# Row maxima of an attention head computed four heads ahead of its scores instead of three

## The chip, the cores and the metric

The kernel runs on one core of a Trainium2 chip. The metric is the time of one execution in device microseconds (us); lower is better. The engines of the core work side by side, each through its own queue in order: PE (matrix multiply, with its weight loads shown as PEld), DVE (vector), ACT (activation functions), POOL (general purpose) and SP, which here issues all DMA transfers. They wait for one another through semaphores.

## What is computed

One transformer-like block on x of 2048 rows and 1024 columns, in fp32. A condition vector gives six modulation rows. Then comes a layer norm, an attention of 32 heads of width 32, a second layer norm and an MLP across the tokens. The attention works on four segments of 512 tokens, each with a causal softmax and with a running memory M, z of the segments before it:

```python
for s in range(N):
    qs, ks, vs = q[:, :, s], k[:, :, s], v[:, :, s]
    logits = jnp.einsum("bhqd,bhkd->bhqk", qs, ks) * scale + mask
    p = _softmax(logits, axis=-1)
    a_dot = jnp.einsum("bhqk,bhkd->bhqd", p, vs)
    pq = phi(qs)
    num = jnp.einsum("bhld,bhde->bhle", pq, M)
    den = jnp.einsum("bhld,bhd->bhl", pq, z)[..., None] + 1e-6
    o = g * (num / den) + (1.0 - g) * a_dot
    pk = phi(ks)
    M = M + jnp.einsum("bhld,bhle->bhde", pk, vs)
    z = z + jnp.einsum("bhld->bhd", pk)
x = x + ga * (o @ wo)
h = _layernorm(x, axis=-1) * (1 + cb) + sb
x = x + gb * mlp_over_tokens(h)
```

The softmax needs the largest logit of each row. This kernel computes the logits twice: once only to take the row maxima, and once more, transposed and with the maximum already subtracted, for the exponentials.

## The kernel before, in words

**Two large stages.** The attention stage lasts until about 1030 us, the MLP stage (lines 874 to 1102) from there to the end; the output product of the attention (line 791) joins them. The change touches the attention stage alone.

**Iterations and heads.** The attention runs over 32 iterations t (list `its`, line 362): two passes over pairs of segments, eight groups of four heads, two segments each. An iteration holds four heads h, so there are 128 heads in all, numbered n = 4t + h. Four kinds of work belong to an iteration:

- `project` (line 378) in four pieces. Pieces 0 and 1 multiply the normed tokens with the key and value weights (PE line 192, tile `nps`), 48 matmuls each. Piece 2 transposes the keys (line 405, `kps`), makes the queries (line 200, `qps`, 24 matmuls), splits both into a high and a low part in the tile `sg` (lines 119 and 122), and sends the parts of heads 0 to 2 with `stack` to the tiles `sk`. Piece 3 sends head 3, makes the values' parts `vp` and calls `memory` (line 441), which reads and updates the running memory (`rd` line 450, `up` line 460).
- `stack` (line 368): three DMAs of one head, lines 374 to 376, `sk<-sg`. There are two sets of `sk`, for even and odd t, so the stack of iteration t overwrites what the scores of iteration t-2 have read.
- `maxima` (line 468): the logits of a head in four matmuls (line 478, tiles `sx`, `sy`, `sz` in the two PSUM banks of tag `s1`), each with a reduction on DVE (line 480) into `mx`. After every second head PE transposes `mx` (line 486, `nmps`, in the only bank of tag `ms`), ACT and DVE make the negated maximum in two parts `nt` (lines 488, 489), and four DMAs write them as two further rows of the `sk` of both heads (line 493, `sk<-nt`).
- `scores` (line 507): four matmuls (lines 515, 518, 521, 522, tile `a`) on all 98 rows of `sk`, so that the maximum is subtracted inside the product; then exponentials on ACT (516, 519, 523), the causal cut on POOL (526), and a high part (528, ACT) and a low part (530, POOL) of the result. `values` (line 532) multiplies these with `vp` (line 544, `pv`) and reduces (547 to 554); after the fourth head the result is transposed (line 559, `ops`, again in the bank `ms`) and stored.

**The loop around the change** (lines 686 to 713) walks over steps n. In a step stand, in this order: the scores of head n, the maxima of head n + LEADS, the values of head n - 2, piece n + 8 of the projections (LEADP), reloads of stored weights and tokens, and planned extras (`plan`, line 590): loads of weights and their split, the norms of later tokens (`token_tile`, line 252), the modulation sums (`mod_late`, line 572, tile `rawm`), the preparation of the output weights. Some of the extras are to be issued on their engine behind a mark of the same step (`behind`, line 499): the last maximum of the step on DVE ("V"), the copy on ACT ("A"), the low part on POOL ("G"). `token_tile` and `mod_late` use the mark "V", which `maxima` sets:

```python
for n in range(-LEADS, 4 * NI + VL):
    at(scores, n)
    at(maxima, n + LEADS)
    at(values, n - VL)
    m = n + LEADP
```

**The order on the engines** isn't this order word for word. The context is opened with `schedule_with_timeline_sim=True` (line 1137): when the kernel is built, the instructions of each engine are put in order by a modelled timeline in which those that come earlier in the program have precedence among those that are ready. On the chip each engine then goes through its list in that fixed order and waits where something is late.

Of the kernel before, what the change touches and what calls it, by code (L numbers as in the profile page):

```python
# [26 lines left out]
SHIFT = 14.0 * math.log(2.0)  # L27
NV = 97
FT = F // P
LEADP, LEADS, NSK = 8, 3, 8  # L30
XB = 4
VL = 2
ML0 = 36
# [2 lines left out]
WOS = 6  # L36
WCT = 5
LEADP = 8
LEADS = 3


def attention_and_mlp(ctx, tc, x, wq, wkv, wo, beta, w1, b1, w2, b2, c, wm_a, wm_b, out):
# [425 lines left out]
    def maxima(t, h):  # L468
# [5 lines left out]
        for tiles in ((0, 1), (2,), (3,)):  # L474
# [4 lines left out]
            for i, o in outs:  # L479
                marks[4 * t + h - LEADS, "V"] = V.tensor_tensor_reduce(  # L480
                    o, o, mask[:, 384 - 128 * i:], 1.0, -3.0e38, op0=ALU.add, op1=ALU.max,
# [111 lines left out]
    def at(f, n):  # L593
        if 0 <= n < 4 * NI:
            f(n // 4, n % 4)
# [89 lines left out]
# [5 lines that stand above are left out]
# [451 lines left out]
```

## Time and profile before

| what | value |
| --- | --- |
| median of 3 runs | 2224.89 us |
| lowest and highest | 2224.09 and 2230.13 us |
| the profiled execution | 2226.6 us, of which its span on the core 2224.9 us |
| granted PE clock over the span | 0.997 |
| DVE, ACT and POOL busy | 1666.7, 1135.7 and 725.8 us |
| DMA | 423.03 MB, mean 190 GB/s |

A row of groups reads: line, engine, operation, out<-in with the program's names, shape, count, then busy time in us and the mean of one in ns, then the idle time of the engine just before them and what ended it. A row of waits reads: who waited, for whom, us in total, times, longest. Times in the timeline count from the start of the span.

### The profile page before, as it was taken

Reading aid. Unit: us, or ns where it says so; the run is one execution under the profiler, and the core shown is the slowest. Engines: PE = TensorE matmul, PEld = TensorE weight load, DVE = VectorE, ACT = ScalarE, POOL = GpSimd, SP = SyncE. Lnnn points to the kernel's source line nnn. Section 1 sums busy time; section 2 is a strip of 40 time slices with the busy share of each in tenths; the row PEclk is TensorE's granted clock in tenths of the full one; section 3 lists DMA queues with packets and bytes.
Section 4 is the critical chain, followed back from the end, with each engine's and each line's share of the span. In section 5 each row is a group of like instructions: output and inputs, shape, how many; then the busy total and the mean of one; then the engine's idle time right before and its main releaser. Section 6 shows DMA issues by size and latency. Waiting matters only on the chain.

```text
span 2224.9 us, 38052 instructions
## 1 busy us (share of the span) xinstructions
PE 2190.3 (98%) x13786; PEld 1881.0 (85%) x13786; DVE 1666.7 (75%) x3762; ACT 1135.7 (51%) x2050; POOL 725.8 (33%) x831
## 2 busy tenths in 40 slices
PE   8999999999999999999999999999999999999999
PEld 5988898888999999888888888888888888888887
DVE  7676777756777777664858766888888886969687
ACT  5486776756666666654636533533334242424232
POOL 2175766646767776663002200033330000000000
PEclk9999999999999999999999999999999999999999
DMA  7666666686556666664754687655556542414134
GB/s 287 192 187 191 175 181 193 189 279 216 170 180 205 188 183 211 193 219 143 231 194 186 226 304 275 243 223 220 204 202 219 206 148 64 145 57 147 57 123 151
DMA packets 175183, 423.03 MB, mean 190 GB/s; under 512 B 17524, under 2 KB 71828, under 8 KB 166036
## 3 DMA queue, kind: packets, MB, share of 16 engines
q1 hardware_dynamic: 174996, 420.61, 57.5%
q8 instruction: 109, 1.79, 0.3%
q14 instruction: 78, 0.64, 0.1%
HBM read 244.62 MB, written 125.06 MB: 166 GB/s over the span
## 4 chain that ended last, share of the span: by engine, by line
PE 87%; DVE 5%; DMA 3%; ACT 2%; POOL 1%; issue 1%; SPq 0%; DVEq 0%; ACTq 0%
PE mx L921 48%; PE nps L192 11%; PE po L791 8%; PE qps L200 7%; PE pv L544 3%; PE a L515 1%; PE sz L478 1%; PE sx L478 1%; DMA sk<-nt 1%; PE up L460 1%; PE a L518 1%; POOL p L530 1%; PE a L522 1%; PE sy L478 1%; PE rd L450 1%
## 5 line engine op out<-in xcount | busy, mean ns | idle before, releaser
L921 PE MATMUL mx<-bU,sp 128*128 128x512 f32 x2352 | 534.3, 389 | 0.9 <-DVE ac L928 0.9
L921 PEld LDWEIGHTS mx<-bU,sp 128*128 128x128 f32 x2352 | 441.3, 188 | 93.4 <-issue 1.3
L119 ACT CAST sp<-wr 128x384 fp32r<-128x384 f32 (+2 forms) x408 | 218.1, 547 | 431.8 <-PE mx L921 349.1
L192 PE MATMUL nps<-wv,h 128*128 128x256 f32 x3072 | 431.2, 283 | 1.6 <-DVE h L122 0.7
L921 PE MATMUL mx<-bA,sp 128*128 128x512 f32 x1764 | 430.5, 389 | 0.0
L530 POOL TENSOR_TENSOR p<-p,ph 128x640 f16<-128x640 f32 x256 | 380.2, 1485 | 138.5 <-ACT ph L528 134.5
L192 PEld LDWEIGHTS nps<-wv,h 128*128 128x128 f32 x3072 | 400.3, 189 | 9.4 <-DVE h L122 2.0
L921 PEld LDWEIGHTS mx<-bA,sp 128*128 128x128 f32 x1764 | 331.2, 188 | 68.7
L122 DVE TENSOR_TENSOR sp<-wr,sp 128x384 fp32r<-128x384 f32 (+2 forms) x408 | 259.8, 648 | 24.7 <-ACT sp L119 24.4
L928 DVE TENSOR_TENSOR ac<-mx,ac 128x512 f32<-128x512 f32 x280 | 189.9, 687 | 85.2 <-PE mx L921 84.1
L200 PE MATMUL qps<-h,wq 128*128 128x512 f32 x768 | 197.9, 400 | 0.0
L528 ACT CAST ph<-p 128x1280 f16<-128x1280 f32 x128 | 161.4, 1261 | 59.7 <-POOL p L526 59.6
L791 PE MATMUL po<-wo,ots 128*128 128x512 f32 x768 | 180.9, 391 | 0.0
L791 PEld LDWEIGHTS po<-wo,ots 128*128 128x128 f32 x768 | 142.7, 188 | 28.7
L200 PEld LDWEIGHTS qps<-h,wq 128*128 128x128 f32 x768 | 141.6, 190 | 27.7
L921 PE MATMUL mx<-bB,sp 128*128 128x512 f32 x588 | 164.0, 389 | 0.0
L526 POOL TENSOR_SCALAR_AFFINE_SELECT p<-p 128x256 f32<-128x256 f32 x256 | 134.1, 529 | 81.8 <-ACT p L523 53.9
L921 PEld LDWEIGHTS mx<-bB,sp 128*128 128x128 f32 x588 | 110.4, 188 | 22.9
L480 DVE CUSTOM_DVE_ANT_0 sz<-sz,mask 128x512 f32<-128x512 f32 x128 | 89.1, 696 | 52.0 <-PE sz L478 49.5
L480 DVE CUSTOM_DVE_ANT_0 sx<-sx,mask 128x128 f32<-128x128 f32 (+1 forms) x256 | 93.7, 366 | 44.1 <-PE sx L478 37.9
L928 DVE TENSOR_TENSOR cc<-mx,cc 128x512 f32<-128x512 f32 x140 | 94.9, 684 | 37.6 <-PE mx L921 37.4
L516 ACT ACTIVATE p<-a,shift 128x512 f32<-128x512 f32 x128 | 88.4, 691 | 41.2 <-PE a L515 40.4
(209 smaller groups left out, 3244.7 us busy)
## 6 DMA issues: line engine op xcount, KB each, us to landing
sk<-sg SPq DMA_DIRECT2D x384, 128.0 KB
wr<-in_w_dram SPq DMA_DIRECT2D x28, 1024.0 KB
wr<-in_w_dram SPq DMA_DIRECT2D x32, 768.0 KB
bstu<-ucd SPq DMA_DIRECT2D x28, 768.0 KB
wsp<-wv SPq DMA_DIRECT2D x32, 512.0 KB
rawm<-in_wm_b_dram SPq DMA_DIRECT2D x32, 512.0 KB
wv<-wsp SPq DMA_DIRECT2D x32, 512.0 KB
pcd<-cc SPq DMA_DIRECT2D x14, 1024.0 KB
```

What stands on the lines that cost most here:

```text
L119: last_hi[0] = A.copy(hi, src)
L122: return lo_eng.tensor_tensor(lo, src, hi.bitcast(F32), op=ALU.subtract)
L192: T.matmul(ps[:, aa], h[:, j, 128 * tt:128 * tt + 128], wt[:, i, o:o + 256], start=(n == 0), stop=(n >= 6 * NK - 2), skip_group_check=True)
L200: T.matmul(ps, wt[:, i, o:o + 128], h[:, j], start=(k + n == 0), stop=(3 * k + n == 3 * NK - 1))
L480: marks[4 * t + h - LEADS, "V"] = V.tensor_tensor_reduce(o, o, mask[:, 384 - 128 * i:], 1.0, -3.0e38, op0=ALU.add, op1=ALU.max, accum_out= ...
L516: A.activation(p32[:, 0:512], b0, AF.Exp, scale=SCALE, bias=shift)
L526: G.affine_select(w, w, pattern=[[0, 2], [1, 128]], compare_op=ALU.is_ge, fill=0.0, base=0, channel_multiplier=-1)
L528: marks[n, "A"] = A.copy(hi, p32)
L530: marks[n, "G"] = G.tensor_tensor(lo[:, c], p32[:, c], hi[:, c], op=ALU.subtract)
L791: T.matmul(ps, os_[:, i, P * ct:P * ct + P], wop[ct, nh][:, j], start=(n == 0), stop=(n == 3 * NK - 1))
L921: T.matmul(ps, ops[q][:, i, P * k:P * k + P], b[:, j], start=(m == 0 and first), stop=(m == 3 * nk - 1), skip_group_check=True)
L928: V.tensor_tensor(d, ps, d, op=ALU.add)
```

## The change

The lead of the maxima over the scores, LEADS, becomes 4:

```diff
@@ -27,7 +27,7 @@
 NV = 97
 FT = F // P
-LEADP, LEADS, NSK = 8, 3, 8
+LEADP, LEADS, NSK = 8, 4, 8
@@ -36,7 +36,7 @@
 LEADP = 8
-LEADS = 3
+LEADS = 4
```

The loop starts one step earlier, at n = -4, and that step holds only the maxima of head 0 and no projection. In every later step stand the maxima of head n + 4 instead of n + 3. No instruction is added or removed; the index of the mark "V" (`4 * t + h - LEADS`, line 480) still names the step in which the maximum stands. Buffers and banks stay as they are.

In the loop's text the maxima of head 0 of an iteration now stand two steps behind piece 2 of its projection (step 4t - 6 against 4t - 4) instead of three. The two heads with a transpose of `mx` (h = 1 and h = 3) fall on the steps in which n leaves 1 and 3 when divided by 4, where they fell on those that leave 2 and 0.

## The prediction

> **What bounds the kernel.** I read the page first, then the two stages, then PE's own waits in the attention stage.
>
> ```profile
> span 2224.9 us, 38052 instructions
> PE 2190.3 (98%) x13786; PEld 1881.0 (85%) x13786; DVE 1666.7 (75%) x3762; ACT 1135.7 (51%) x2050; POOL 725.8 (33%) x831
> PE 87%; DVE 5%; DMA 3%; ACT 2%; POOL 1%; issue 1%; SPq 0%; DVEq 0%; ACTq 0%
> PE mx L921 48%; PE nps L192 11%; PE po L791 8%; PE qps L200 7%; PE pv L544 3%; PE a L515 1%; PE sz L478 1%; PE sx L478 1%; DMA sk<-nt 1%; PE up L460 1%; PE a L518 1%; POOL p L530 1%; PE a L522 1%; PE sy L478 1%; PE rd L450 1%
> ```
> ```profile
> 60.00:1030.00 970.00, 950.20 (x8249) 864.27 (x8249) 688.30 (x2048) 636.92 (x1136) 612.63 (x717) 0.99 0.65 195
> 1030.00:2225.00 1195.00, 1190.41 (x5267) 984.75 (x5265) 934.52 (x1626) 466.77 (x862) 99.61 (x65) 1.00 0.51 181
> ```
> ```profile
> PE a L515 <- DMA sk<-nt: 4.1, 5, 1.4
> PE up L460 <- DVE am L454: 3.8, 3, 3.5
> PE a L521 <- ACT p L516: 2.4, 3, 1.0
> PE sy L478 <- DVE mx L480: 1.9, 2, 1.2
> ...
> PE sx L478 <- DMA sk<-sg: 0.2, 1, 0.2
> ```
>
> The columns of the two stretches (from the view of busy time by stretch) are length, then PE, PEld, DVE, ACT, POOL busy, the granted clock, the DMA share and GB/s. PE is the bound throughout: in the MLP stage it idles 1195.0 - 1190.4 = 4.6 us, in the attention stage 970.0 - 950.2 = 19.8 us. DVE, ACT and POOL have room in both (688, 637 and 613 us of 970). So the change can't shorten the work; it can only remove or add places where PE, going through its list in a fixed order, stands still. The waits that it aims at, scores that wait for the maxima's rows (`a L515 <- DMA sk<-nt`), are 4.1 us in five places of 128. The chain that ended last gives the same transfer 1% of the span, 22 us, but counts the whole flight of a transfer, with work of PE beside most of it; I keep it as the outer bound of a gain.
>
> **How far ahead the maxima really are.** The change names the program's order; the trace shows the engines' order.
>
> ```profile
> L478 PE MATMUL sx<-sk x256: 218/325/522, 62.4 to 988.7; 96*128 96x128 f32 x128
> L515 PE MATMUL a<-sk x128: 391/400/505, 98.5 to 1017.7; 98*128 98x512 f32 x128
> ```
>
> One head takes (1017.7 - 98.5) / 127 = 7.24 us. The first head's maxima run 98.5 - 62.4 = 36.1 us ahead of its scores, five heads; the last head's 1017.7 - 988.7 = 29.0 us, four heads. So the lead of three in the text is a lead of four to five on the engine. What holds the maxima from running still earlier is the arrival of the stacked queries and keys, as iteration 19 shows, with SP's queue first and PE's behind it:
>
> ```profile
> 613.51 0.68 SPq L374 DMA_DIRECT2D sk<-sg  x1
> 614.32 0.64 SPq L375 DMA_DIRECT2D sk<-sg  x1
> 615.41 2.65 SPq L493 DMA_DIRECT2D sk<-nt  x4
> 618.10 0.59 SPq L376 DMA_DIRECT2D sk<-sg  x1
> ```
> ```profile
> 623.74 0.22 PE L478 MATMUL sx<-sk 96*128 96x128 f32 x1
> ```
> ```profile
> 129.27 3.26 DMA sk<-sg
> ```
> ```profile
> 491.71 3.58 DMA sk<-sg
> ```
>
> The third stack DMA of head 0 is issued at 618.10; by the two pieces of the chain such a DMA lands 3.3 to 3.6 us after its issue, so at about 621.5, and the first maxima matmul starts at 623.74: 2.2 us of room. Between the first two and the third, SP issued four `sk<-nt` of an earlier pair, 2.65 us; the two kinds of transfer share the queue.
>
> **Part by part.**
>
> (a) *Scores no longer wait for `nt`.* The maxima of heads 1 to 3 can come up to one head, 7.24 us, earlier; their stacks land sooner than they are needed. Of the 4.1 us, the mean wait is 4.1 / 5 = 0.8 us. Bounds: 0 (SP's queue, below, decides when `nt` leaves) and -4.1. I take -3: four of five gone.
>
> (b) *Maxima of head 0 move up against their stack.* Room is 2.2 us, the move 7.24 us: followed to the letter, PE would stand 5 us in each of 31 iterations, 155 us. That is no likely end, because the list is made from a modelled timeline that puts other matmuls first while a stack isn't there; before, such waits came to 0.2 us in one place. But the matmul now stands as close behind its DMA as the model believes, 31 times, and the model doesn't see what SP is held by:
>
> ```profile
> SPq L493 <- ACT nt L488: 31.6, 12, 9.5
> ...
> SPq L374 <- PE a L522: 7.5, 7, 2.2
> ```
>
> SP stands for `nt` 12 times, up to 9.5 us, with the stacks of the next iteration, weight loads and stores queued behind it. With `nt` one head earlier in that queue, whoever is late there delays the stacks, and PE waits for those, with all matmuls of its list behind the waiting one. Bounds: 0 and 31 waits of the mean that the other maxima transfer shows, 0.8 us: 25 us. Between them I take a third of the places, 10 x 0.8 = +8.
>
> (c) *The bank `ms` is used in bunches.* Its users in turn were: `nmps` (steps with remainder 0 and 2), `ops` (1), two `rd` and one `up` (3). After, `nmps` stands in the steps of `ops` and of `rd`, `rd`, `up`, and the other two are empty. Each user must wait until DVE or ACT has read the one before; the row `up <- DVE am`, 3.8 us, is this wait. Bounds: 0 (the model spreads them) and one turn more in 32 iterations, the reading of `rd` in this row, 0.42 us, and a wait of the mean above, 0.8 us:
>
> ```profile
> L454 DVE TENSOR_TENSOR am<-rd,rdd 128x256 f32<-128x256 f32 x48 | 20.2, 420 | 0.7
> ```
>
> so at most 32 x 1.22 = 39 us. Nearest is the wait seen, and I let it double: +4.
>
> (d) *DVE work behind the mark "V".* The 32 modulation sums and eight token norms go one head later in DVE's list, because their mark is now the maximum of the next head. The timeline shows such a sum, 1.32 us, right behind its mark:
>
> ```profile
> 367.55 0.70 DVE L480 CUSTOM_DVE_ANT_0 sz<-sz,mask 128x512 f32<-128x512 f32 x1 [2.08 <-PE sz L478]
> ...
> 368.45 1.32 DVE L573 SCALAR_TENSOR_TENSOR rawm<-rawm,scb 128x1024 f32<-128x1024 f32 x1
> ```
>
> Their loads get 7 us more to land, but their three buffers (tag `raw`, shared with the weight loads) are held as much longer. Where this has mattered is the largest stop of the stage:
>
> ```profile
> 449.51 1.92 DVE L573 SCALAR_TENSOR_TENSOR rawm<-rawm,scb 128x1024 f32<-128x1024 f32 x1 [1.55 <-DMA rawm<-in_wm_b_dram]
> ```
> ```profile
> 455.29 1.00 PE L460 MATMUL up<-v,pk 128*128 128x132 f32 x3 [3.48 <-DVE am L454]
> ```
> ```profile
> 450.00:460.00 10.00, 6.53 (x47) 5.92 (x46) 9.08 (x20) 6.25 (x13) 5.03 (x9) 0.69 1.03 361
> 460.00:470.00 10.00, 10.00 (x60) 8.35 (x59) 5.53 (x16) 4.60 (x8) 7.27 (x7) 0.80 0.91 323
> ```
>
> A modulation sum waited for its load, two weight splits stood behind it, then the reading of the memory's bank for which `up` waits, and PE stood for 3.48 us. After that the granted clock was 0.69 and 0.80 over two stretches of 10 us, which loses 10 x 0.31 + 10 x 0.20 = 5.1 us more. One such stop costs 8.6 us. The new order may lose this one (-8.6) or make another (+8.6); no row says which, so I take 0 and keep both.
>
> ```profile
> 130.00:140.00 10.00, 9.22 (x68) 8.06 (x67) 7.21 (x13) 8.63 (x15) 6.87 (x9) 0.83 0.99 264
> ```
>
> Short waits can lower the clock too: here PE was busy for 9.2 of 10 us, idle for 0.8, and the clock was 0.83, a loss of 1.7 us. The Trainium skill, "TensorE: Matmul & The Clock Gate", section "What's actually happening", ties the fall to half the clock to an idle window of about 3.4 us. The stop at 455 us agrees with it (3.48 us); the stretch at 130 us doesn't. By that rule new waits of 0.8 us would cost no clock, and term (b) would stay +8; by this stretch they can cost as much again, which I leave to the upper end.
>
> (e) *Start and end.* The step added in front holds nothing new: by the trace, the maxima of five heads stand ahead of the first scores already. At the end PE has the output product beside the last heads (`po` runs in the same stretch), so an earlier last maximum frees nothing. The token reloads behind the last `nt` of iteration 14 leave one head earlier in SP's list; PE's waits have no row for them. I take 0 for all.
>
> Sum: -3 + 8 + 4 + 0 + 0 = +9 us on the span, 2224.9 to 2233.9. The profiled execution lies 1.7 us above both its span and the median of the runs (2226.6 against 2224.9 and 2224.89), so a median of 2224.9 + 9 = 2234 us, 0.4% slower. Its own range, with (b) and (c) from half to twice: 2224.9 - 3 + 6 = 2228 to 2224.9 - 3 + 24 = 2246.
>
> **The rivals.**
>
> *R1, faster.* All `nt` waits go (-4.1), the model spaces the stacks as well as it did before, and with the mark of DVE one head later the sum at 449 us finds its load, so the stop at 455 us isn't there (-8.6): 2224.9 - 12.7 = 2212 us. For it: both rows are real and the second hangs on DVE's order, which the mark moves. Against it: what brought the load late is the DMA share, 1.03 in that stretch, which stays. With the stop alone gone, 2216.
>
> *R2, nothing.* The maxima run four to five heads ahead already and arrive when their stacks do; the edit changes a precedence that seldom decides, and waits only move from one place to another. 2225 us. This is also the case in which the change does not do what it says. For it: idle time is 19.8 us in all. Against it: the marks and the bank order do change, and the order of every engine is made anew.
>
> *R3, much slower.* SP is the place: `nt` earlier in its queue makes it stand longer for ACT and DVE, the stacks behind it come late in all iterations, and PE waits there long enough to lose the clock. Ten stops of half the size of the one at 455 us, 4.3 us each, are 43 us: 2268 us. It decides when the three stack DMAs of head 0 leave more than the 2.2 us of room later than now. For it: 2.65 us of `nt` between two stack DMAs; against it: 0.2 us of such waits so far.
>
> *R4, the bank `ms` alone:* (c) at its bound without (b), 2225 - 3 + 39 = 2261 us; for it the single bank, against it that other matmuls fill PE while a bank is read.
>
> **How the numbers follow.** The forecast has 0.34, R1 0.31, R2 0.26, R3 and R4 together 0.09. A measurement of this kernel can tell about 0.3% from no change, 6.7 us: under 2218.2 is faster, over 2231.6 slower. R1 lies under the first almost whole: faster 0.31. The forecast's range begins at 2228, so some of its chance is within the bound, and some of R2's lies outside above; these make up for one another: same 0.27, slower 0.42. The range goes from R1's end, 2211, to the middle between the forecast's upper end, 2246, and R3's 2268, about 2256; R3, R4 and the part of R1 with the full 22 us are left out.
>
> **What would show it.** (a) The row `a <- sk<-nt` falls from 4.1 to about 1 us, and the lead of the last head's maxima grows from 29.0 us towards 36. (b) A row `sx <- sk<-sg` of several us appears in PE's waits, or SP's waits for `nt` grow over 31.6 us; if it stays under 1 us, (b) is wrong. (c) `up`, `rd` or `nmps` waiting for DVE over 8 us together; under 4 us and (c) is wrong. (d) The stretch around 450 us: whether PE stands there and the clock falls. PE idle in the attention stage should grow from 19.8 us to near 29; if it shrinks, R1 holds. The MLP stage should keep its 1195 us; a change there would mean that the cost isn't in the attention at all.

## The result, and the profile after

The changed kernel takes 2238.56 us (median of 6 runs, 2236.66 to 2241.59); the kernel before, on the same chip, 2225.33 us (6 runs, 2223.67 to 2230.13). The ratio is 1.0057, with a 95% interval of 1.0043 to 1.0070. The forecast was 2234 us, 9 us more; it became 13.2 us more. The direction and the range hold, but the terms of the sum don't: several were off in both directions and made up for one another.

The page after (span, busy time by engine, the chain that ended last by engine and by line):

```profile
span 2239.7 us, 38045 instructions
PE 2198.5 (98%) x13786; PEld 1886.1 (84%) x13786; DVE 1664.3 (74%) x3762; ACT 1131.8 (51%) x2050; POOL 714.9 (32%) x831
...
PE 87%; DVE 5%; ACT 3%; DMA 2%; POOL 2%; issue 1%; SPq 0%; DVEq 0%; ACTq 0%
PE mx L921 47%; PE nps L192 11%; PE po L791 8%; PE qps L200 7%; PE pv L544 3%; PE sx L478 1%; PE sz L478 1%; PE a L515 1%; PE up L460 1%; DMA sk<-sg 1%; POOL p L530 1%; PE sy L478 1%; PE a L518 1%; PE a L522 1%; PE rd L450 1%
```

The span grew by 14.8 us. PE's idle time went from 2224.9 - 2190.3 = 34.6 to 2239.7 - 2198.5 = 41.2 us, its busy time up by 8.2 us with the same 13786 matmuls: part of the loss is standing, part is slower matmuls. A lower clock accounts for some 3 of these 8.2 us (last section); no view here assigns the rest. In the chain `sk<-nt` has left the list, and `sk<-sg` has come in.

The two stages after, by stretch (columns as before), PE's waits in the attention stage, and the lead of the maxima:

```profile
60.00:1030.00 970.00, 943.28 (x8168) 856.85 (x8169) 679.20 (x2033) 630.38 (x1129) 598.18 (x713) 0.99 0.64 193
1030.00:2240.00 1210.00, 1205.18 (x5347) 996.89 (x5346) 941.70 (x1643) 469.95 (x870) 103.15 (x69) 1.00 0.51 181
```
```profile
PE sx L478 <- DMA sk<-sg: 6.1, 6, 2.2
PE a L515 <- DMA sk<-nt: 3.6, 1, 3.6
```
```profile
L478 PE MATMUL sx<-sk x256: 220/328/523, 62.9 to 991.6; 96*128 96x128 f32 x128
...
L515 PE MATMUL a<-sk x128: 389/400/781, 99.0 to 1020.2; 98*128 98x512 f32 x128
```

Between 60 and 1030 us PE stands 26.7 us instead of 19.8. Beyond, to the end of the span, it stands 4.5 us in both kernels. The first matmul of the MLP starts at 1167.8 us instead of 1153.3, so 14.5 of the 14.8 us are lost ahead of it. The row `sx <- sk<-sg`, 0.2 us before, is 6.1 us. The row `a <- sk<-nt`, 4.1 us in five places, is 3.6 us in one. The row `up <- DVE am`, 3.8 us before, is below the rows that the view shows. The lead of the last head's maxima is 1020.2 - 991.6 = 28.6 us, where it was 29.0: the earlier place in the text gave the last head no earlier start on PE.

Where in the stage is it lost? I took from both traces the time at which PE had done the same amount of matmul work, counted at steady intervals. The times are those of the changed kernel, and five places matter: 102 to 169 us (+7.8 us), 280 to 395 us (+5.5), 440 to 510 us (-5.1, a gain), 510 to 569 us (+3.5, the one wait for `nt`) and 948 to 1007 us (+3). The first place, then the former stop at 455 us, after:

```profile
120.00:130.00 10.00, 9.88 (x79) 8.14 (x75) 5.83 (x24) 5.90 (x13) 3.00 (x3) 1.00 0.09 18
130.00:140.00 10.00, 5.78 (x21) 3.76 (x21) 5.35 (x15) 10.00 (x20) 5.10 (x6) 0.72 0.88 260
140.00:150.00 10.00, 10.00 (x76) 9.53 (x76) 7.26 (x21) 5.53 (x9) 7.59 (x11) 0.77 0.98 302
...
450.00:460.00 10.00, 9.39 (x87) 8.87 (x86) 7.98 (x19) 7.96 (x15) 6.91 (x9) 1.00 0.91 252
```

Between 130 and 140 us PE now stands for 4.2 us (0.8 before), and the clock costs 2.8 + 2.3 = 5.1 us in two stretches (1.7 before). The stop at 455 us with its low clock is gone. PE still stands 2.3 us in small pieces between 450 and 470 us (3.5 before), so the gain there is the 5.1 us above and not the 8.6 us that the stop cost by the prediction's sum. What stands ahead of the new stop is the first of the eight token norms. These are the same five steps of it in the timeline, before and after: DVE's statistics, ACT's normalisation, PE's transpose, ACT's split of the next value weights, and the first `nps` matmul of iteration 4 that uses them:

```profile
108.10 1.28 DVE L127 BATCH_NORM_STATS2 st<-gaw 128x6 f32<-128x512 f32 x2
...
113.34 1.25 ACT L239 ACTIVATE gaw<-gaw,mv 128x1024 f32<-128x1024 f32 x1 [1.15 <-DVE mv L238]
...
117.22 0.60 PE L260 MATMUL hpl<-ident,gaw 128*128 128x128 f32 x4
...
132.93 1.23 ACT L119 CAST wv<-rawv 128x512 fp32r<-128x512 f32 x2
...
134.09 2.27 PE L192 MATMUL nps<-wv,h 128*128 128x256 f32 x9
```
```profile
113.06 1.28 DVE L127 BATCH_NORM_STATS2 st<-gaw 128x6 f32<-128x512 f32 x2
...
121.39 1.25 ACT L239 ACTIVATE gaw<-gaw,mv 128x1024 f32<-128x1024 f32 x1
...
126.90 1.04 PE L260 MATMUL hpl<-ident,gaw 128*128 128x128 f32 x8
...
138.64 1.13 ACT L119 CAST wv<-rawv 128x512 fp32r<-128x512 f32 x2
...
141.14 1.63 PE L192 MATMUL nps<-wv,h 128*128 128x256 f32 x6
```

The delay grows from 5 us to 10 us and then shrinks again: the statistics start 4.96 us later (behind the maximum of head 7 instead of head 6), the normalisation 8.05, the first half of the transposes 9.68. Before, the second half followed 5 us behind the first; after, both come in one go, so the norm's last work on ACT (`hix`) is 6.0 us later, at 131.9 instead of 125.9 us. The `nps` matmuls of iteration 4 come 7 us later, while those of iteration 3 end at 115.0 us instead of 116.9. So the stretch without any `nps` grows from 17 to 26 us. In it PE lives on queries, scores and maxima, and after 130 us these run out:

```profile
132.13 0.33 PE L521 MATMUL a<-sk 98*128 98x128 f32 x1 [0.91 <-ACT p L516]
...
133.55 0.27 PE L486 MATMUL nmps<-ident,mx 128*8 128x128 f32 x1 [0.92 <-ACT ot L561]
134.04 0.55 PE L515 MATMUL a<-sk 98*128 98x512 f32 x1 [0.21 <-ACT p L519]
134.99 0.69 PE L518 MATMUL a<-sk 98*128 98x384 f32 x1 [0.41 <-ACT p L523]
136.65 0.47 PE L521 MATMUL a<-sk 98*128 98x128 f32 x1 [0.97 <-ACT p L516]
...
139.43 0.77 PE L478 MATMUL sx<-sk 96*128 96x128 f32 x2 [0.67 <-DMA sk<-sg]
```

No wait is over 1 us, and no single row is to be blamed: a view of waits alone would miss this place. But five of the six rows name ACT, 3.4 of the 4.2 us that PE stands here, and by the row of the stretch above ACT is busy for all 10 us.

### The profile page after: what moved, and what is told of

Same layout as the page of the kernel before. It is cut to its first block, busy times and chain, and to the rows that moved or that the text cites. A ratio compares the mean times of both kernels' runs of the same rounds, so it can differ in the third digit from the quotient of the medians.

```text
span 2239.7 us, 38045 instructions
## 1 busy us (share of the span) xinstructions
PE 2198.5 (98%) x13786; PEld 1886.1 (84%) x13786; DVE 1664.3 (74%) x3762; ACT 1131.8 (51%) x2050; POOL 714.9 (32%) x831
## 4 chain that ended last, share of the span: by engine, by line
PE 87%; DVE 5%; ACT 3%; DMA 2%; POOL 2%; issue 1%; SPq 0%; DVEq 0%; ACTq 0%
PE mx L921 47%; PE nps L192 11%; PE po L791 8%; PE qps L200 7%; PE pv L544 3%; PE sx L478 1%; PE sz L478 1%; PE a L515 1%; PE up L460 1%; DMA sk<-sg 1%; POOL p L530 1%; PE sy L478 1%; PE a L518 1%; PE a L522 1%; PE rd L450 1%
## 5 line engine op out<-in xcount | busy, mean ns | idle before, releaser
L530 POOL TENSOR_TENSOR p<-p,ph 128x640 f16<-128x640 f32 x256 | 376.7, 1473 | 142.6 <-ACT ph L528 137.8
L526 POOL TENSOR_SCALAR_AFFINE_SELECT p<-p 128x256 f32<-128x256 f32 x256 | 128.1, 506 | 104.6 <-ACT p L523 61.4
L523 ACT ACTIVATE p<-a,shift 128x384 f32<-128x384 f32 x128 | 74.4, 581 | 72.6 <-PE a L522 71.7
```

What stands on the lines that cost most here:

```text
L523: A.activation(p32[:, 896:1280], b2_[:, 0:384], AF.Exp, scale=SCALE, bias=shift)
L526: G.affine_select(w, w, pattern=[[0, 2], [1, 128]], compare_op=ALU.is_ge, fill=0.0, base=0, channel_multiplier=-1)
L530: marks[n, "G"] = G.tensor_tensor(lo[:, c], p32[:, c], hi[:, c], op=ALU.subtract)
```

## The experiments

The trace left two candidates for the net loss. One is the mark "V": the token norms and the modulation sums follow the last maximum of their step on DVE, which is now that of the next head (term (d), taken as 0). The other is the stacks' wait on PE (term (b)). To tell them apart I moved the one without the other. All ratios are against the kernel before on the same chip. Its median beside these runs lay between 2225.33 and 2229.49 us, so it is the ratios that compare, not the medians.

| run | what differs | median us | ratio, 95% interval | first MLP matmul, us |
| --- | --- | --- | --- | --- |
| the change | | 2238.56 | 1.0057 (1.0043 to 1.0070) | 1167.8 |
| e1 | old mark for norms and sums | 2228.57 | 1.0000 (0.9990 to 1.0010) | 1153.7 |
| e6 | old mark for the norms alone | 2226.81 | 0.9997 (0.9987 to 1.0007) | 1152.5 |
| e12 | old mark for the first norm alone | 2240.33 | 1.0048 (1.0030 to 1.0066) | 1163.8 |
| e2 | lead 3, norms and sums late | 2228.98 | 1.0001 (0.9990 to 1.0013) | 1153.7 |
| e4 | lead 3, maxima ahead of scores | 2233.72 | 1.0018 (1.0007 to 1.0029) | 1161.4 |
| e5 | old mark, lead 3 for head 0, else 4 | 2223.42 | 0.9973 (0.9961 to 0.9984) | 1149.4 |
| e13 | e5 with the norms late | 2246.14 | 1.0081 (1.0065 to 1.0097) | 1167.2 |
| e8 | old mark, lead 3 for heads 0 and 1 | 2236.10 | 1.0043 (1.0028 to 1.0059) | 1161.3 |
| e7 | the change, value weights fetched early | 2238.48 | 1.0055 (1.0039 to 1.0070) | 1163.8 |
| e11 | e7, their split without its mark | 2234.95 | 1.0028 (1.0015 to 1.0040) | 1163.2 |
| e10 | the change, first norm in another bank | 2245.04 | 1.0077 (1.0058 to 1.0095) | 1172.3 |
| e9 | the change, `nmps` in another bank | 2241.10 | 1.0063 (1.0046 to 1.0079) | 1166.6 |

### e1: the lead of four with the old mark

```diff
-                marks[4 * t + h - LEADS, "V"] = V.tensor_tensor_reduce(
+                marks[4 * t + h - 3, "V"] = V.tensor_tensor_reduce(
```

> Lead four, but the mark of a step is the maximum of head n + 3 again, as before the change, so that the token norms and modulation sums stand where they stood. Theory A (the late extras): the 8 us lost between 102 and 169 us come back, since the first token norm and with it the weights of the third group leave as early as before: 2225 + 5 = about 2230 us. Theory B (maxima of head 0 gated by their stacks): 2238 us, the sx waits stay near 6 us. Theory C (any new order costs): 2232 to 2245 us, with the loss at other places.

Measured: 1.0000 (0.9990 to 1.0010). The loss is gone, and the stretch from 130 to 140 us with it, while PE's wait for the stacks is larger than in the changed kernel:

```profile
130.00:140.00 10.00, 8.53 (x72) 7.09 (x71) 8.27 (x20) 9.01 (x16) 5.98 (x6) 1.00 1.00 298
```
```profile
PE sx L478 <- DMA sk<-sg: 8.2, 8, 2.4
```

What follows: all of the net loss hangs on where the marked work stands. The stacks' wait is real, but it isn't what makes the changed kernel slower than before: with 8.2 us of it this kernel is even. What pays for it are the waits for `nt`, which are not among its rows any more, and the low clock at 455 us: PE still stands 3.2 us between 450 and 470 us, in four pieces, but the clock stays at 1.00.

### e6: the norms alone with the old mark

The modulation sums keep the new mark; the token norms go behind the maximum of the step before.

```diff
-                if (n, e) in marks:
-                    s.enter_context(tc.issue_after(marks[n, e].ins))
+                k = (n - 1, "V") if e == "v" else (n, e)
+                if k in marks:
+                    s.enter_context(tc.issue_after(marks[k].ins))
...
-              6 * i + 3, lambda r, i=i: token_tile(8 + i), "V")
+              6 * i + 3, lambda r, i=i: token_tile(8 + i), "v")
```

> The changed kernel (lead four), with the old mark, the maximum of head n + 3, for the eight token norms alone; the 32 modulation sums keep the new one. Theory A1 (the norms hold up the weights through the shared buffers): most of what the old mark gave comes back, ratio 1.000 to 1.002, and no low clock near 135 us. Theory A2 (the modulation sums do it): the ratio stays at 1.005 to 1.007. The sx waits stay at 4 to 9 us in both.

Measured: 0.9997 (0.9987 to 1.0007), with 9.5 us of stacks' wait:

```profile
PE sx L478 <- DMA sk<-sg: 9.5, 8, 2.7
```

What follows: of the marked work, the eight token norms carry the loss; the 32 modulation sums, one head later, cost nothing that can be measured as long as the norms come early.

### e12: the first norm alone with the old mark

```diff
-              6 * i + 3, lambda r, i=i: token_tile(8 + i), "v")
+              6 * i + 3, lambda r, i=i: token_tile(8 + i), "v" if i == 0 else "V")
```

> The changed kernel with the first of the eight token norms alone back behind the earlier maximum (that of head 6); the other seven and all modulation sums as changed. Theory F (the first norm carries the whole loss): start as before, scores of head 4 near 123 us, ratio 0.999 to 1.001. Rival E (all eight cost a little): ratio 1.003 to 1.005.

Measured: 1.0048 (1.0030 to 1.0066), what the rival expected. The start is mended, but a stop stands later:

```profile
130.00:140.00 10.00, 8.62 (x73) 7.24 (x72) 8.34 (x20) 8.82 (x16) 6.16 (x6) 1.00 0.97 299
...
370.00:380.00 10.00, 6.27 (x29) 5.15 (x28) 7.45 (x15) 4.47 (x9) 7.00 (x6) 0.94 0.67 204
```
```profile
376.11 2.08 DVE L574 SCALAR_TENSOR_TENSOR rawm<-rawm,scb 128x1024 f32<-128x1024 f32 x1 [2.55 <-DMA rawm<-in_wm_b_dram]
```
```profile
378.86 3.13 PE L192 MATMUL nps<-wv,h 128*128 128x256 f32 x13 [3.73 <-DVE sg L122]
```

This stop isn't of the kind of the one at 130 us. It is of the kind of the one at 455 us in the kernel before: a modulation sum waits for its load, a split stands behind it on DVE, and PE waits for that. The load was issued at 368.0 us here and at 359.2 us in e6, where the stop is absent; the norm's two stores, which stand ahead of it in SP's list, were 11 and 12 us later than in e6.

What follows: I had put the whole loss on the first norm, because the stop at 130 us is the largest single place. That was wrong. With the other seven late most of the loss is still there, at other places. That they cost it one by one is not shown: the largest place hangs on a modulation sum as well.

### e2: the late extras alone, with a lead of three

```diff
-              6 * i + 3, lambda r, i=i: token_tile(8 + i), "V")
+              6 * i + 4, lambda r, i=i: token_tile(8 + i), "V")
...
-        later(n, lambda j=j: mod_fetch(j), n + (2 if j < 8 else 1), lambda r, j=j: mod_late(j, r), "V")
+        later(n, lambda j=j: mod_fetch(j), n + (3 if j < 8 else 2), lambda r, j=j: mod_late(j, r), "V")
```

> Lead three as before, but the token norms and modulation sums are planned one step later, so that they stand behind the maximum of head n + 4. Theory A: the start loses its 8 us without any change of the lead: about 2233 us, with PE idle and a low clock near 135 us. Theory B: 2225 us, no sx waits. Theory C: 2226 to 2235 us, with no place of its own.

Measured: 1.0001 (0.9990 to 1.0013). The kernel before doesn't mind its norms one maximum later. It isn't a clean mirror of e1, since moving the norm by a step also lets the weights of group 2 be fetched ahead of it; the stretch from 130 to 140 us is worse than before, its clock falls only in the next 10 us (0.83), and the stop at 455 us is gone here too:

```profile
130.00:140.00 10.00, 7.19 (x64) 5.84 (x62) 7.52 (x21) 8.43 (x16) 5.23 (x6) 1.00 0.93 270
```

What follows: a norm that comes late doesn't have to cost. Its statistics start at 114.3 us here, later than in the changed kernel, and `hix` stands at 132.0 us. But the first part of the value weights of group 2 is split at 125.6 and 127.5 us (138.6 in the changed kernel), and `nps` of iteration 4 starts at 126.7 us, ahead of its place in the kernel before. So this run doesn't say what a late norm costs at a lead of three with its weights late too.

### e7, e10, e11: which link carries the late norm to PE

Three links were taken out in turn of the kernel with the change. In e7 the value weights of group 2 are fetched at step 2, ahead of the norm:

```diff
-            later(n + n0, lambda g=g, kind=kind, part=part: fetch_part(g, kind, part),
+            later(2 if g == 2 and kind == "v" else n + n0, lambda g=g, kind=kind, part=part: fetch_part(g, kind, part),
```

> The changed kernel with one thing different: the value weights of the third group are fetched in step 2, ahead of the first token norm, instead of in steps 3 and 4. Theory A1 with the shared buffers as its way: the fetch leaves near 73 us instead of 129 us, the stop between 130 and 140 us is gone, and 7 to 8 us come back: ratio 1.002 to 1.003. If the norm's work on ACT and DVE itself is what holds PE up, nothing comes back: 1.0057.

Measured: 1.0055 (1.0039 to 1.0070), as the change alone. The weights were on their way at 72.6 us already, and `nps` of iteration 4 still began at 140.9:

```profile
130.00:140.00 10.00, 6.37 (x22) 3.88 (x20) 5.35 (x17) 10.00 (x19) 5.55 (x7) 0.67 0.65 167
```

So it isn't the fetch, nor the three buffers `raw`. In e10 the transposes of the first norm leave the two banks that they share with the scores:

```diff
-            ps = bank("s2", 2, f"hpl{tt}_{half}")
+            ps = bank("ms", 1, f"hpl{tt}_{half}") if tt == 8 else bank("s2", 2, f"hpl{tt}_{half}")
```

> The changed kernel, but the transposes of the first token norm (hpl of token tile 8) go into the bank ms, not into the two banks s2 that the scores use. Theory S (the late norm sits between the scores of head 3 and of head 4 in the banks s2, so the scores of head 4 start at 129.5 us instead of 122.8): scores of head 4 near 123 us, stretch 130 to 140 us with PE busy for over 9 us, ratio 1.000 to 1.002. Rival N (the norm costs by its own load on DVE, ACT and the weight split behind it, the banks do not matter): scores of head 4 near 123 or not, but nps of iteration 4 still starts at about 141 us, PE busy for under 7 us in 130 to 140, ratio 1.005 to 1.006.

Measured: 1.0077 (1.0058 to 1.0095). The scores of head 4 start at 116.9 us instead of 129.5, as theory S wanted, and still PE stands, and `nps` of iteration 4 comes at 142.6:

```profile
130.00:140.00 10.00, 6.39 (x60) 4.76 (x59) 5.97 (x22) 10.00 (x21) 6.73 (x9) 0.79 0.69 187
```
```profile
142.61 1.70 PE L192 MATMUL nps<-wv,h 128*128 128x256 f32 x7
```

Theory S falls: with the shared banks out of the way `nps` is as late as in the changed kernel, and scores done early are only missing later. In e11 the weights of e7 are also split without waiting for the mark on ACT:

```diff
-                  n + n1, lambda r, g=g, kind=kind, part=part: split_part(g, kind, part, r), "A")
+                  n + n1, lambda r, g=g, kind=kind, part=part: split_part(g, kind, part, r),
+                  "" if g == 2 and kind == "v" else "A")
```

> The kernel of the run with the value weights of group 2 fetched early, and their split no longer behind the ACT mark of its step (the copy of head 4, which comes late when the scores of head 4 do). Theory M (that mark passes the lateness on to the weights of iteration 4): nps of iteration 4 starts at about 132 us or earlier, PE is busy for over 9 us in 130 to 140, ratio 1.000 to 1.003, although the scores of head 4 stay late. Rival S alone (the late scores themselves leave PE without work): nps of iteration 4 starts early and runs out elsewhere before 160 us, ratio 1.004 to 1.006.

Measured: 1.0028 (1.0015 to 1.0040), half of the loss. Now `nps` of iteration 4 starts at 129.0 us and PE is full to 140 us, but the stop comes 15 us later, with a stack that is late:

```profile
130.00:140.00 10.00, 10.00 (x84) 9.84 (x83) 6.15 (x16) 9.32 (x18) 4.96 (x5) 1.00 0.81 226
140.00:150.00 10.00, 8.48 (x89) 7.47 (x87) 7.92 (x29) 7.83 (x13) 7.29 (x11) 1.00 0.59 146
150.00:160.00 10.00, 7.93 (x29) 6.39 (x30) 8.17 (x25) 5.60 (x13) 7.62 (x9) 0.57 0.33 109
```
```profile
150.59 0.47 PE L478 MATMUL sx<-sk 96*128 96x128 f32 x2 [2.11 <-DMA sk<-sg]
```

The mark on the weight split is one link, worth up to half. Its ratio lies within what theory M expected, but its stop is the one that the rival expected. The other half isn't pinned to a link. ACT is the likely one: in order, it has the norm's 8 scalings, its casts, the splits and the exponentials in one list, and it is busy for all 10 us between 130 and 140 us in the changed kernel, in e7 and in e10. No run moved ACT's work alone, so this is argued and not shown.

### e5 and e13: the fastest kernel, and the norms in it

e5 is e1 with a lead of three kept for head 0 of an iteration, whose stack comes last:

```diff
-        at(maxima, n + LEADS)
+        for k in (3, 4):
+            if (n + k) % 4 == 0 if k == 3 else (n + k) % 4:
+                at(maxima, n + k)
```

> Lead four for heads 1 to 3 of an iteration, lead three for head 0, with the mark of head n + 3. Theory A: the same as the kernel with the old mark alone, about 2230 us. Theory B: the sx waits fall from 6.1 us to under 1 us, and the time is 5 to 8 us below that of the kernel with the old mark alone: near 2225 us if A holds too, near 2231 us if it does not.

Measured: 0.9973 (0.9961 to 0.9984), faster than both kernels. PE's waits for the stacks halve against e1 (they don't fall under 1 us, as theory B asked), waits for `nt` don't come back, and PE stands 17.0 us in the stage, less than in any other of these kernels:

```profile
60.00:1030.00 970.00, 952.96 (x8284) 865.63 (x8285) 692.99 (x2053) 634.51 (x1138) 608.92 (x718) 1.00 0.65 196
```
```profile
PE sx L478 <- DMA sk<-sg: 3.9, 5, 1.4
```

e13 puts the eight norms of this kernel, and nothing else, behind the maximum of head n + 4:

```diff
-                if (n, e) in marks:
-                    s.enter_context(tc.issue_after(marks[n, e].ins))
+                k = (n + 1, "V") if e == "v" else (n, e)
+                if k in marks:
+                    s.enter_context(tc.issue_after(marks[k].ins))
...
-              6 * i + 3, lambda r, i=i: token_tile(8 + i), "V")
+              6 * i + 3, lambda r, i=i: token_tile(8 + i), "v")
```

> The fastest kernel so far (lead 3 for head 0, 4 for heads 1 to 3, ratio 0.9973) with one thing changed: the eight token norms stand behind the maximum of head n + 4, as in the changed kernel, while the modulation sums keep the mark of head n + 3. Theory A (the place of the norms costs 0.4 to 0.6%, whatever the lead): ratio 1.001 to 1.004, PE out of projection work between 130 and 141 us, nps of iteration 4 starting at 138 us or later. Rival Z (what costs is chance in the order of each new program, and the norms were only one occasion): ratio 0.995 to 0.999.

Measured: 1.0081 (1.0065 to 1.0097), more than theory A expected and far from the rival. The stop at 130 us is back with all its marks; `nps` of iteration 4 starts at 140.4 us, in e5 at 132.1:

```profile
130.00:140.00 10.00, 6.38 (x24) 3.90 (x23) 5.20 (x15) 10.00 (x19) 5.63 (x7) 0.59 0.90 259
```
```profile
140.42 1.95 PE L192 MATMUL nps<-wv,h 128*128 128x256 f32 x8
```

What follows: the place of the norms decides in a second arrangement too. Late to early is worth 1.0057 to 0.9997 in the first pair and 1.0081 to 0.9973 in the second.

### e8, e4, e9: the lead and the order by themselves

e8 keeps the lead of three for heads 0 and 1 with the old mark; e4 is the kernel before with the maxima ahead of the scores in each step; e9 is the changed kernel with `nmps` in the banks of the maxima, so that `ms` has one user less.

```diff
-        at(maxima, n + LEADS)
+        for k in (3, 4):
+            if ((n + k) % 4 < 2) == (k == 3):
+                at(maxima, n + k)
```

> Lead three for heads 0 and 1 of an iteration, four for heads 2 and 3, old mark. Theory B (maxima too close to their stacks): the sx waits that the kernel with lead three for head 0 alone still has, 3.9 us in five places, fall under 1 us, and the time is 2 to 4 us below it: ratio 0.995 to 0.997. If those waits belong to other causes they stay, and the ratio is 0.997 to 1.000.

```diff
-        at(scores, n)
         at(maxima, n + LEADS)
+        at(scores, n)
```

> Lead three, but within a step the maxima of head n + 3 stand ahead of the scores of head n; no step of any work changes. A look at what a new order alone does. Theories A and B: 2225 us within 3 us, since neither the marks nor the distance to the stacks move. Theory C: a loss of 5 us or more, or a gain, at no place that A or B name.

```diff
-        ps = bank("ms", 1, f"nmps{t}_{h}")
+        ps = bank("s1", 2, f"nmps{t}_{h}")
```

> The changed kernel, with the transpose of the maxima in the two banks s1 of the logits instead of in the only bank ms. Term (c) of the prediction (the bank ms is used in bunches): the waits of up, rd, ops and nmps for DVE and ACT, about 6 us together, fall to near 1 us, and the time falls by 4 us: ratio near 1.004. If the bank costs nothing: 1.0057, or more where the transposes now hold up the logits.

Measured: 1.0043, 1.0018 and 1.0063. Waits for `nt`, one row of each, in that order:

```profile
PE a L515 <- DMA sk<-nt: 4.0, 3, 1.9
```
```profile
PE a L515 <- DMA sk<-nt: 4.5, 3, 2.1
```
```profile
PE a L515 <- DMA sk<-nt: 7.1, 3, 3.3
```

And in e8 its stacks' wait:

```profile
PE sx L478 <- DMA sk<-sg: 1.8, 2, 1.2
```

e8 was a miss: its stacks' wait is down to 1.8 us, and yet it is slower than e1 with 8.2, with the waits for `nt` back and PE standing 24.9 us in the stage against 22.0 in e1. The stacks' wait alone doesn't order these kernels. In e4 a swap of two lines that shortens nothing costs 0.2%: each new program gets a new order on every engine, and some per mille come or go with it. e9 gives no support to term (c): with `ms` relieved, nothing is gained.

## Why the prediction was right, and where it wasn't

**(a) `nt` waits gone, -3.** In the changed kernel only -0.5: one wait of 3.6 us, at 529 us, took the place of five short ones. In e1 and e5 the row is gone from the view, so the mechanism holds. The remaining wait comes from the token reloads (`h<-hT`) that term (e) put at nothing. The second part of `nt` starts on DVE at 519.57 us and takes 0.28 us; its transfers stand behind three reloads in SP's list and leave 3 us later:

```profile
519.57 0.28 DVE L489 SCALAR_TENSOR_TENSOR nt<-nmps,nt 8x128 fp32r<-8x128 f32 x1
```
```profile
519.52 3.22 SPq L359 DMA_DIRECT2D h<-hT  x3
522.84 2.76 SPq L493 DMA_DIRECT2D sk<-nt  x4
```

**(b) Stacks gate the maxima of head 0, +8.** The wait was right, and the size nearly: 0.2 to 6.1 us, in 6 places instead of the 10 assumed, at 1.0 us each instead of 0.8. The reason given, that SP is held by `nt`, isn't borne out: SP's waits for `nt` fell from 31.6 to 23.8 us, and in the 10 us ahead of the two longest waits (2.2 us at 390 us, 1.7 at 952) SP issues no `sk<-nt`. In the kernels with the old mark it is 8.2 and 9.5 us. The last head's lead stayed at 28.6 us; the 36 us named as a sign for (a) didn't come. That the stacks hold it there is likely, but no run shows it.

**(c) Bank `ms`, +4.** Wrong by its own sign: `up` waiting for `am`, 3.8 us, all but vanished, the waits of `up`, `rd` and `nmps` for DVE come to 3.6 us together (`rd <- pv` 1.5 us, `up <- pk` 1.3, four small ones), under the 4 us set as its sign, and e9 gained nothing. The text had taken the 3.8 us for a wait at the bank and doubled it, but 3.48 of them are the stop at 455 us, which (d) puts down to a late sum. The term is about 0.

**(d) Work behind the mark, 0 with 8.6 either way.** Here the sum was mis-sized. The text said that the new order may lose the stop at 455 us or make another, and both happened: that stop went (5.1 us gained there), and another came at 130 us (4.2 us of standing and 5.1 us of clock, 6.8 us more than before there) and smaller ones later. The sums behind the mark, which the text worked out, cost nothing (e6); the eight norms, which it named and did not cost, carry the net loss: 1.0057 against 0.9997, 0.6% or about 13 us. The step that failed was the pricing of a norm as DVE work alone. It is a chain over DVE, ACT, PE, POOL and SP: the mark's 5 us were 8 us at its first work on ACT and 6 us at its last, and ACT, full from 130 to 140 us, kept PE waiting. The reading that the stop at 455 us agrees with an idle window of 3.4 us was wrong too, as the last section shows.

**(e) Start and end, 0.** The MLP stage kept its time (14.5 of 14.8 us were lost ahead of it). But the token reloads made the wait of 3.6 us under (a), and the start of the stage, about which the text said that the step in front holds nothing new, is where most was lost, through (d).

**The sum and the rivals.** That +9 came near +13 is luck: (c), 4 too high, the norms, missing, and the lost stop, missing, nearly cancel. What the traces assign, -0.5 for (a), 5.9 for (b), -5.1 for the lost stop and 6.8 for the new one, is about 7 of the 14.8 us of the span; the rest lies in smaller places. R1's second half did happen, against the reason given: the stop at 455 us went, and the DMA share there fell from 1.03 to 0.91. Nor does the share decide it: in e2 it is 1.06 in that stretch, and there is no stop. R3's mechanism, ten long stops at the stacks, isn't there: the longest is 2.2 us.

**What stays open.** What a late norm costs at a lead of three when its weights are late too (e2 had them early), which links carry the half that e11 leaves, and how the other seven norms share the loss. That the norms' place carries the net loss rests on two pairs of kernels with the same sign. Chance in the order isn't ruled out as a part of it, since e8 loses 0.4% with its norms in the old place. e5 is the fastest kernel measured, but e8, with one head's lead different, is 0.7% slower: e5 is a good order that was found, and no rule about leads follows from it.

## What to carry to other kernels

When an index that places one stage is changed, list everything that hangs on it, such as marks behind which other work is issued, and move or hold each on purpose: here the same lead costs 0.6% with the mark moved along and nothing with it held. Price an extra by its whole chain over the engines, and ask what PE lives on until its end comes out. Where a builder orders the instructions anew, compare pairs that differ in one thing, in two arrangements, before blaming the largest new wait.

## What the runs showed of the hardware

The granted clock fell without a long stop, and inside one before it was over. In the changed kernel no wait of PE between 130 and 140 us is over 0.97 us, but together they are 4.2 of 10 us, and the clock was 0.72 there and 0.77 in the next 10 us. In the kernel before, PE stood from 451.8 to 455.3 us, and the clock was already at half from 454 us on:

```profile
452.00:453.00 1.00, 0.00 (x0) 0.00 (x0) 1.00 (x1) 1.00 (x3) 1.00 (x2) 1.00 0.99 340
453.00:454.00 1.00, 0.00 (x0) 0.00 (x0) 1.00 (x3) 0.71 (x2) 0.51 (x1) 0.92 1.05 426
454.00:455.00 1.00, 0.00 (x0) 0.00 (x0) 1.00 (x6) 0.00 (x0) 0.00 (x0) 0.50 1.00 373
```

A mean of 0.92 between 453 and 454 us puts the fall at about 453.8 us, 2.0 us after PE stopped. But the share of waiting in a stretch doesn't order the kernels: between 130 and 140 us e1 was idle for 1.5 us and the clock stayed at 1.00, there and in the next 10 us, while before, with 0.8 us, it was 0.83. What sets the fall is not settled here. The Trainium skill, "TensorE: Matmul & The Clock Gate", section "What's actually happening", says that the gate goes by how busy PE has been recently, and names an idle window of about 3.4 us for the fall; by these rows PE need not stand for a whole such window. Summed over the stretches with a lower clock, this cost 10.2 us after (the two at 130 us and three of 1.7 us, near 390, 530 and 953 us) and 6.8 us before, so some 3 us of the loss are the clock's (for a part of these stretches PE stood anyway).
